# A recurrent attention and a leaky-ReLU layer on one core: the first quad's instructions and loads in a new order

## The chip, the core and the metric

The kernel runs on one core of a Trainium2 chip. The metric is device time in microseconds (us) of one execution, lower is better. The core has five engines with a queue each: TensorE (PE in the profile; its weight loads are shown apart, as PEld), VectorE (DVE), ScalarE (ACT), GpSimd (POOL) and SyncE (SP), which here only issues DMAs. Each queue is worked off in its own order; between queues an instruction waits on semaphores for the data that it reads and for the buffers that it writes.

## What is computed

Four batches of eight heads, 768 steps, head size 48. Each head keeps a 48 x 48 state that decays by a gate and takes up an outer product per step; its outputs, with the heads side by side, are the rows of x (3072 x 384), which go through two matrix products with a leaky ReLU between.

```python
f = 1.0 / (1.0 + np.exp(-f_logit))
for t in range(S):
    state = f[:, :, t, :, None] * state + np.einsum('bhd,bhe->bhde', k[:, :, t], v[:, :, t])
    y[:, :, t] = np.einsum('bhd,bhde->bhe', q[:, :, t], state)
x = y.transpose(0, 2, 1, 3).reshape(B * S, H * D)
h = x @ w_in                      # 384 x 2048
out = np.maximum(0.01 * h, h) @ w_out   # 2048 x 384
```

## The kernel before

The 768 steps are cut into six chunks of 128. A chunk of one batch is a unit (24 of them, number 4c + b); the four units of a chunk are a quad, and all its data for q, k, v and f is loaded at once, 128 partitions of 1536 fp32 values, 768 KB. Within a chunk the recurrence becomes matrix products: running sums of the logarithm of the gate give decay factors; k and q are scaled by them (k by the exponential of the sum, q by that of its negative), turned so that the head dimension lies on partitions (kT and qT), multiplied to scores, masked to a triangle, and multiplied with v; what earlier chunks left is added by a product with the state.

**The stages of a quad**, as the helpers name them:

- gate: `g_exp`, `g_ln` (ACT, two halves of the heads), `g_sum`, `g_cast`, `g_pe` (the sum over partitions on TensorE), `g_add`, then the factors `g_em` and `g_a` (ACT, into the single buffers `em_t` and `a_t`) and `g_end`;
- scaling on DVE: `g_k` and `g_q`; then either DMA moves and DMA transposes (`kq_dma`, `t_dma`) or turns on TensorE (`t_pe`, `t_out`) to kT and qT; v is cast (`cast_v`) and moved (`v_dma`);
- `score_pe`, `mask`, `mix_pe`, `y_out` per unit, and the state: `state_pe`, `state_dve`, `state_pool`;
- x is turned, by `x_pe` and `x_out` (TensorE and a copy) or by `x2_dma` (a DMA transpose of two units);
- the layer: `up4` (three matmuls 128x512 for one of 16 groups of columns of w_in, all four units) with `up4_act` (the leaky ReLU on ACT), and `down` (four matmuls 128x384, a quarter of the sum over 2048) with `put` and the stores. For quad 0 the first product runs in two halves of two units each, as `up` (six matmuls 128x256, two groups of columns) with `up_act`.

**The first quad** has functions of its own, named `q_...` (lines 221 to 323). Its gate sums are made on TensorE with 32-row matmuls (`q_gate32`), the decay factors leave PSUM through ACT (`q_decay_b`, into `emT` and `aT`), k and q are cast and turned unscaled (`q_k_cast`, `q_q_cast`, `q_turn_pe`), and scaled on the way out of PSUM (`q_k_mul`, `q_q_mul`). v is picked into natural order by matmuls (`q_pick`, `q_v_out`). Half of the score blocks go through a DVE mask, the other half through an ACT copy (`q_wf_act`) and a triangle select on POOL (`q_mask_pool`). `idle_pe(n, bank)` issues n matmuls on zeros.

**What sets the order.** Nothing is scheduled by a compiler. Line 60 turns automatic scheduling off, and the calls from line 512 to line 1360 are one list; each engine gets its instructions in the order of this list. The list was found by a search, apart from the calls of the first quad, which stood by hand. The eight PSUM banks are given as numbers in the calls: an operation that fills a bank waits until the last reader of that bank is done.

**Loads and their queues.** f of quad 0 comes in six pieces on the ACT and SP queues; k, q and v of quad 0 on SP (lines 83, 84, 512). All other loads of q, k, v and f are `load_all` on SP, in the order of the list. The weights go through POOL's queue, with a cast from fp32 to bf16: w_in in two halves of its columns (`load_w_in`), w_out in four pieces (`load_w_out`). SP's queue and POOL's queue are served side by side by the same 16 DMA engines. Two helpers hold a queue back: `gate(t, src)` has POOL write one element of a buffer from `src`, so that the load into that buffer comes after it, and `touch(what)` has POOL read one element of a loaded tile, so that POOL goes on only when that load has landed:

```python
gate(fqs[1], v_bs[1][:, 0, 0:1])      # L599: f of quad 1 after the first v of quad 0
touch('q')                            # L532: ahead of both w_in loads on POOL
touch('k1')                           # L665: ahead of w_out pieces 1 to 3 on POOL
```

fqs, kqs and qqs are pairs of buffers, of which quad c uses number c % 2; `v_raws` is one buffer. f of quad 2 goes into the buffer that quad 0 used.

Of the kernel before, what the change touches and what calls it, by code (L numbers as in the profile page):

```python
# [16 lines left out]
def kernel(  # L17
# [10 lines left out]
    nc = tc.nc  # L28
# [55 lines left out]
    load_all(qq, q)  # L84
# [437 lines left out]
    idle_pe(4, 7)  # L522
    q_turn_pe(khq, 0, 4)
    q_decay_b(0, emT, 1.0, 0, 0)
    q_decay_b(1, emT, 1.0, 1, 0)
    q_gate32(1, 0, 1, 2, 3)
    q_decay_b(0, aT, -1.0, 0, 0)
    q_k_mul(0, 0, 0, 4)
    q_turn_pe(khq, 1, 5)
    q_k_mul(0, 1, 0, 4)  # L530
    q_decay_b(3, emT, 1.0, 3)
    touch('q')  # L532
    q_q_cast(V, 1)
# [48 lines left out]
    q_q_mul(1, 1, 1, 6)
    q_pick(2, 7)
    q_v_out(A, 3, 5)
    q_mix_pe(1, 4)
    q_mix_pe(0, 3)
    q_v_out(V, 2, 7)
    q_score_pe(1, 1, 1, 2)
    y_out(A, 1, 4)
    y_out(V, 0, 3)  # L590
    q_back_pe(3, 6)
    state_pe(0, 5)
    q_mask(1, 1, 0, 1)
    q_wf_act(1, 1, 1, 2)
    x_pe(1, 0)
    x_pe(0, 7)
    q_score_pe(0, 1, 4, 3)
    load_w_out(0)
    gate(fqs[1], v_bs[1][:, 0, 0:1])  # L599
    q_back_out(A, 3, 6)  # L600
    x_out(V, 1, 0)
    state_pe(1, 2)
    x_out(V, 0, 7)
    q_back_pe(2, 1)
    q_mask_pool(1, 1, 1)
    q_wf_act(0, 1, 1, 3)
    q_mask(0, 1, 0, 4)
    state_pe(3, 0)
    order_pe(6)
    load_all(fqs[1], f_logit, 1)  # L610
    load_all(kqs[1], k, 1)
    q_state_dve(0)
    up(0, 7, 7)
# [48 lines left out]
    up_act(1, 7, 1)
    up_act(1, 0, 4)
    q_state_pool(3)
    touch('k1')  # L665
    g_sum(V, 1, 2)
    g_sum(V, 1, 3)
    up_act(0, 2, 5)
    up_act(1, 3, 2)
    g_cast(V, 1)  # L670
    g_pe(1, 6)
    g_add(1, 1, 6)
    g_em(1, 1)
    load_w_out(1)
    g_add(1, 0, 6)
    up(1, 6, 1)
    g_a(1, 0)
    down(3, 0, 4)
    g_em(1, 0)
    load_all(fqs[0], f_logit, 2)  # L680
    g_a(1, 1)
    up_act(1, 6, 1)
    load_all(fqs[1], f_logit, 3)
    g_k(V, 1, 2)
    g_k(V, 1, 3)
    g_q(V, 1, 0)
    down(2, 0, 5)
    up(1, 5, 2)
    load_w_out(2)
    load_w_out(3)  # L690
    g_q(V, 1, 1)
    down(1, 1, 7)
    down(0, 1, 3)
    g_end(1, 6)
    up_act(1, 5, 2)
    t_pe(1, 0, 1, 0)
    down(3, 1, 4)
    t_out(A, 1, 0, 1, 0)
    t_pe(1, 1, 0, 6)
    g_k(V, 1, 0)  # L700
    g_k(V, 1, 1)
    t_pe(1, 0, 0, 2)
    t_out(A, 1, 0, 0, 2)
    down(0, 2, 3)
    g_q(V, 1, 3)
    g_q(V, 1, 2)
    t_pe(1, 1, 1, 0)
    t_out(A, 1, 1, 1, 0)
    down(2, 1, 5)
    down(3, 2, 4)  # L710
    t_out(V, 1, 1, 0, 6)
    score_pe(6, 0, 6)
    mask(6, 0, 0)
    mask(6, 1, 6)
    g_exp(2, 1)
    g_exp(2, 0)
    q_state_pool(1)
    cast_v(G, 1, 1)
    q_state_pool(0)
    cast_v(G, 1, 0)  # L720
    v_dma(1, 2)
    v_dma(1, 1)
    score_pe(4, 2, 1)
# [12 lines left out]
    g_ln(2, 1)
    mix_pe(6, 1)
    mask(7, 1, 0)
    g_exp(3, 1)
    v_dma(1, 0)  # L740
    g_ln(2, 0)
    v_dma(1, 3)
# [4 lines left out]
    down(3, 3, 4)  # L747
    mix_pe(4, 2)
    put(A, 1, 7)
    kq_dma(1, 0, 1)  # L750
    y_out(A, 4, 2)
    y_out(A, 6, 1)
    mix_pe(5, 3)
    y_out(A, 5, 3)
    state_pe(5, 7)
    mix_pe(7, 0)
    y_out(A, 7, 0)
    x_pe(4, 2)
    down(2, 3, 5)
    kq_dma(1, 0, 3)  # L760
    kq_dma(1, 0, 2)
    kq_dma(1, 0, 0)
    x_pe(5, 3)
    load_all(kqs[0], k, 2)
    x_out(A, 4, 2)
    x_pe(7, 0)
    x_out(V, 7, 0)
    put(A, 3, 4)
    x_out(A, 5, 3)
    load_all(v_raws[0], v, 2)  # L770
    x_pe(6, 1)
    x_out(V, 6, 1)
    g_ln(3, 1)
    state_pe(4, 2)
    state_pe(6, 6)
    cast_v(G, 2, 0)
    state_dve(4)
    state_pe(7, 4)
    g_pe(2, 0)
    g_add(2, 1, 0)  # L780
    g_exp(3, 0)
    up4(1, 0, 1)
    up4_act(1, 0, 1)
    state_dve(7)
    state_dve(5)
    up4(1, 10, 2)
    state_pool(7)
    cast_v(G, 2, 1)
    up4(1, 1, 3)
    g_em(2, 1)  # L790
    g_add(2, 0, 0)
    up4_act(1, 1, 3)
    g_end(2, 0)
    g_k(V, 2, 2)
    up4(1, 6, 1)
# [24 lines left out]
    up4(1, 15, 6)  # L820
    put(V, 2, 5)
    g_sum(V, 3, 2)
    down(5, 0, 7)
    kq_dma(2, 0, 0)
    up4(1, 8, 2)
    g_q(V, 2, 1)
    g_q(V, 2, 2)
    g_q(V, 2, 0)
    up4_act(1, 4, 3)
    up4(1, 5, 5)  # L830
    up4_act(1, 5, 5)
    up4_act(1, 13, 1)
    up4(1, 14, 0)
    kq_dma(2, 0, 1)
    up4(1, 11, 3)
    g_sum(V, 3, 3)
    up4_act(1, 11, 3)
    g_q(V, 2, 3)
    up4_act(1, 14, 0)
    up4_act(1, 8, 2)  # L840
    up4(1, 9, 5)
    up4_act(1, 9, 5)
    state_pool(4)
    t_pe(2, 1, 0, 1)
    down(4, 0, 3)
    t_out(V, 2, 1, 0, 1)
    t_pe(2, 1, 1, 0)
    t_out(A, 2, 1, 1, 0)
    g_cast(G, 3)
    g_pe(3, 2)  # L850
    g_add(3, 0, 2)
    up4_act(1, 15, 6)
    g_add(3, 1, 2)
    g_a(3, 0)
    g_em(3, 0)
    state_pool(5)
    state_pool(6)
    g_end(3, 2)
    down(4, 1, 3)
    out_dma(2)  # L860
    kq_dma(2, 0, 3)
    kq_dma(2, 0, 2)
    down(5, 1, 7)
    g_a(3, 1)
    g_em(3, 1)
# [24 lines left out]
    load_all(fqs[0], f_logit, 4)  # L890
# [500 lines left out]
```

## Time and profile before

| | us |
|---|---|
| median of three runs | 183.94 |
| lowest and highest run | 181.56, 184.01 |
| the profiled execution | 184.06 |
| its span, from first to last instruction | 182.3 |
| TensorE busy | 169.2 (93% of the span) |
| ACT busy | 116.1 (64%) |
| DVE busy | 108.6 (60%) |
| POOL busy | 49.8 (27%) |
| granted TensorE clock, mean | 0.99 |
| HBM read, written | 25.17 MB, 4.72 MB |

Busy time of TensorE is not work at its peak: the end of a matmul is modelled, and matmuls overlap, so a group of n takes less than n times the mean of one. The chain of waits shows a group at the rate at which it really passes. An instruction that waits is not busy; the trace gives the idle time before it and what ended it. A DMA is shown with its issue (on SPq or POOLq) and the time from issue to landing. In the queries, PE L472 is `up`, L482 `up4`, L490 `down`, L417 the scores, L428 and L431 the two halves of `mix_pe`, L439 `state_pe`, L462 `x_pe`, L399 `t_pe`, L252 `q_pick`; on ACT L477 and L486 are the activations of `up` and `up4`, L328 is `g_exp`; on DVE L267 is `q_k_mul` and `q_q_mul`; L73 is any `load_all`, L179 `load_w_in`, L184 `load_w_out`.

### The profile page before, as it was taken

How to read it: one execution, taken by the hardware profiler on the slowest of the kernel's cores; microseconds unless marked ns; L12 is line 12 of the kernel's file. 1: busy time of each engine (PE TensorE's matmuls, PEld its weight loads, DVE VectorE, ACT ScalarE, POOL GpSimd, SP SyncE). 2: the span in 40 equal slices, each digit the busy share in tenths (PEclk: the TensorE clock that was granted, in tenths of full speed). 3: DMA queues.
4: the chain of work that ended last, by engine and by line, in shares of the span. 5: the costliest groups of instructions: out<-in, count | busy, mean ns of one | idle time of the engine just before them, and what ended most of it. 6: DMA issues, size and time to landing. Idle time of an engine off the chain costs nothing.

```text
span 182.3 us, 3982 instructions
## 1 busy us (share of the span) xinstructions
PE 169.2 (93%) x1546; PEld 107.4 (59%) x1546; DVE 108.6 (60%) x229; ACT 116.1 (64%) x211; POOL 49.8 (27%) x99
## 2 busy tenths in 40 slices
PE   7589999939999999979989999999999999999992
PEld 5375889717584555665545675556755566555561
DVE  7679942892699789759566895666780057400020
ACT  2878498955898999385987179861566921076302
POOL 8377205630015333001840176120006500000000
PEclk9999999978999999999999999999999999999999
DMA  5998999999797058998698797889477884371004
GB/s 157 309 234 155 210 296 327 312 217 327 212 338 231 29 170 154 329 330 246 205 139 185 235 331 253 187 156 324 110 192 249 172 208 137 61 281 64 4 0 173
DMA packets 55171, 37.61 MB, mean 206 GB/s; under 512 B 19569, under 2 KB 53873, under 8 KB 55153
## 3 DMA queue, kind: packets, MB, share of 16 engines
q1 hardware_dynamic: 53216, 33.82, 65.8%
q0 software_dynamic: 1376, 3.15, 9.7%
q10 hardware_dynamic: 560, 0.39, 0.7%
q8 instruction: 12, 0.20, 0.5%
q14 instruction: 7, 0.05, 0.1%
HBM read 25.17 MB, written 4.72 MB: 164 GB/s over the span
## 4 chain that ended last, share of the span: by engine, by line
PE 63%; DMA 22%; ACT 5%; SPq 3%; DVE 3%; POOL 1%; issue 1%; DVEq 0%; ACTq 0%; POOLq 0%
PE ps L490 29%; PE ps L482 24%; DMA kq<-in_k_dram 15%; DMA w_out_b<-in_moe_w_out_dram 5%; PE ps L417 3%; DMA kTs<-kh 3%; ACT gT L238 2%; PE ps L431 2%; PE ps L428 2%; PE ps L399 2%; PE ps L439 1%; PE ps L462 1%; SPq L392 1%; SPq L382 1%; SPq L69 1%
## 5 line engine op out<-in xcount | busy, mean ns | idle before, releaser
L490 PE MATMUL ps<-w_out_b,gT 128*128 128x384 bf16 x384 | 71.9, 330 | 2.9 <-DMA w_out_b<-in_moe_w_out_dram 2.9
L486 ACT ACTIVATE gT<-ps 128x512 bf16<-128x512 f32 x80 | 44.6, 606 | 19.2 <-PE ps L482 18.3
L482 PE MATMUL ps<-xQ,w_in 128*128 128x512 bf16 x240 | 54.4, 379 | 0.6 <-ACT gT L486 0.6
L490 PEld LDWEIGHTS <-gT 128*128 128x128 bf16 x384 | 35.4, 98 | 25.4 <-issue 4.1
L482 PEld LDWEIGHTS <-w_in 128*128 128x128 bf16 x240 | 26.8, 113 | 23.4 <-issue 0.8
L421 DVE TENSOR_TENSOR wm<-ps,ut 128x512 bf16<-128x512 f32 x40 | 25.3, 684 | 22.0 <-PE ps L417 21.6
L147 ACT CAST xn<-ps 128x384 bf16<-128x384 f32 x20 | 9.0, 485 | 21.8 <-PE ps L431 19.5
L149 DVE COPY osb<-ps 128x384 f32<-128x384 f32 x11 | 5.9, 554 | 23.2 <-PE ps L490 21.2
L320 POOL CAST sb<-sf 64x192 bf16<-64x192 f32 x40 | 16.2, 404 | 9.7 <-DVE sf L314 5.6
L453 POOL TENSOR_TENSOR sf<-sf,a_end 128x192 f32<-128x192 f32 x16 | 9.6, 600 | 30.8 <-PE ps L482 15.8
L149 POOL CAST vQ<-v_raw 128x768 bf16<-128x768 f32 x9 | 7.6, 847 | 20.0 <-DMA qh<-qhQ 18.0
L368 DVE TENSOR_TENSOR khQ<-kq,em_t 128x384 bf16<-128x384 f32 x20 | 11.3, 600 | 2.5 <-DMA kq<-in_k_dram 2.0
L147 ACT COPY osb<-ps 128x384 f32<-128x384 f32 x13 | 6.1, 486 | 10.2 <-PE ps L490 10.2
L472 PE MATMUL ps<-xQ,w_in 128*128 128x256 bf16 x96 | 12.1, 273 | 0.2
L368 DVE TENSOR_TENSOR qhQ<-qq,a_t 128x384 bf16<-128x384 f32 x20 | 11.8, 619 | 0.3 <-DMA qq<-in_q_dram 0.3
L336 DVE TENSOR_TENSOR fq<-fq 128x384 f32<-128x384 f32 x15 | 8.6, 572 | 5.5 <-ACT fq L332 5.2
L472 PEld LDWEIGHTS <-w_in 128*128 128x128 bf16 x96 | 10.2, 114 | 1.1 <-issue 0.7
L352 DVE TENSOR_TENSOR fq<-fq,ps 128x768 f32<-128x768 f32 x10 | 9.4, 953 | 2.3 <-PE ps L346 1.8
L328 ACT ACTIVATE fq<-fq 128x768 f32<-128x768 f32 x10 | 8.3, 851 | 0.7 <-DMA fq<-in_f_logit_dram 0.7
L360 ACT ACTIVATE a_t<-fq 128x768 bf16<-128x768 f32 x10 | 8.5, 853 | 0.0
L356 ACT ACTIVATE em_t<-fq 128x768 bf16<-128x768 f32 x10 | 8.5, 851 | 0.0
L477 ACT ACTIVATE gT<-ps 128x512 bf16<-128x512 f32 x16 | 8.3, 600 | 0.0
(98 smaller groups left out, 188.3 us busy)
## 6 DMA issues: line engine op xcount, KB each, us to landing
kq<-in_k_dram SPq DMA_DIRECT2D x6, 768.0 KB, 7.2
qq<-in_q_dram SPq DMA_DIRECT2D x6, 768.0 KB, 9.8
fq<-in_f_logit_dram SPq DMA_DIRECT2D x5, 768.0 KB, 9.5
v_raw<-in_v_dram SPq DMA_DIRECT2D x5, 768.0 KB, 7.3
out_dram<-osb SPq DMA_DIRECT2D x4, 768.0 KB, 4.6
kh<-khQ SPq DMA_DIRECT2D x20, 128.0 KB, 3.6
v_b<-vQ SPq DMA_DIRECT2D x20, 96.0 KB, 2.2
w_in<-in_moe_w_in_dram POOLq DMA_DIRECT2D x2, 768.0 KB, 9.3
```

What stands on the lines that cost most here:

```text
L147: eng.copy(out=out, in_=in_)
L149: eng.tensor_copy(out=out, in_=in_)
L320: nc.gpsimd.tensor_copy(out=state_b[b][r, :, e * D:(e + 1) * D], in_=state_f[b][r])
L336: eng.tensor_add(t[:, :, j, :], t[:, :, j, :], t[:, :, j - 1, :])
L352: nc.vector.tensor_add(t, t, x[:, :, None, :].to_broadcast([128, 4, 4, D]))
L368: eng.tensor_mul(out.rearrange("p (j g) d -> p j g d", j=4)[:, :, h, 0:D], raw[:, h].rearrange("p e j d -> p j e d"), by[:, h].rearrange(" ...
L421: nc.vector.tensor_mul(wms[e][u % R_WM], bank(bk).rearrange("p (i n) -> p i n", i=P2), ut[:, None, :].to_broadcast([128, P2, 128]))
L453: nc.gpsimd.tensor_mul(sf, sf, a_ends[c % 2][:, :, b:b + 1].to_broadcast([128, P2, D]))
L472: nc.tensor.matmul(bank(bk)[:, i * 256:(i + 1) * 256].rearrange("p (a n) -> p a n", a=2), w_in_p[ff // 8][:, kk, ff // 4 % 2, :, ff % 4], ...
L482: nc.tensor.matmul(bank(bk).rearrange("p (a n) -> p a n", a=B), w_in_p[ff // 8][:, kk, ff // 4 % 2, :, ff % 4], xQs[c % R_XT][:, :, kk, :] ...
L486: nc.scalar.activation(g_piece(c, ff), bank(bk), AF.Prelu, alpha=0.01)
L490: nc.tensor.matmul(bank(bk)[:, 0:KD], g_part(u, ff), w_out_b[:, ff, :], start=(ff == 0), stop=(ff == NF - 1))
```

## The change

The whole list of calls is replaced by another one, in which the calls of the first quad stand in a searched order too. The set of operations stays nearly the same; apart from the order, bank numbers change, and some copies and casts change their engine. What differs in kind:

- Loads of quad 0 go in the order k, v, q. After them come f of quad 1 and f of quad 2, which stood far later in the list; k, q and v of quad 1 follow.
- The gate ahead of f of quad 1 reads `ident`, a constant, and not the first v. `touch('k')` takes the place of `touch('q')`; `touch('k1')` is gone.
- w_in is loaded in four quarters of its columns, in the order 0, 2, 1, 3. Of w_out, piece 1 is loaded first, then 0, 2 and 3.
- `g_exp` of quad 1, first half, stands on ACT ahead of the four `q_wf_act`; the gate work of quads 1 and 2 runs up to their sums while `up` of quad 0 runs.
- All four `q_mix_pe` stand ahead of the first `up`; before, two of them did.
- `idle_pe` issues 58 matmuls, where before it issued 36.
- x of quad 3 is turned by two `x2_dma`, where before by four `x_pe` and `x_out`.
- The description of the change also says that q of quad 2 is turned on TensorE. In both lists that is two calls `t_pe(2, 1, ...)`; the list of before has them on lines 844 and 846.

The diff, cut to its core:

```diff
     load_all(kq, k)
-    load_all(qq, q)
...
     def load_w_in(g):
-        w = FF // 2
-        nc.gpsimd.dma_start(out=w_in_b[g],
+        w = FF // 4
+        nc.gpsimd.dma_start(out=w_in_b[g // 2][:, :, g % 2 * w:g % 2 * w + w],
                             in_=moe_w_in.rearrange("(a p) n -> p a n", p=128)[:, :, g * w:(g + 1) * w])
...
     load_all(vq, v)
+    load_all(qq, q)
+    idle_pe(24, 7)
     q_exp_act(0)
+    q_exp_act(1)
     q_ln_act(0)
-    q_exp_act(1)
-    idle_pe(24, 7)
+    idle_pe(15, 7)
     q_gate32(0, 0, 1, 2, 3)
     q_ln_act(1)
+    gate(fqs[1], ident[:, 0:1])
+    touch('k')
+    q_gate32(1, 0, 1, 2, 3)
     q_k_cast(V, 0)
-    q_k_cast(G, 1)
+    load_all(fqs[1], f_logit, 1)
...
+    load_all(fqs[0], f_logit, 2)
...
+    q_v_cast(G, 0)
+    q_decay_b(3, emT, 1.0, 3, None)
+    q_decay_b(2, emT, 1.0, 2, None)
...
+    q_v_cast(A, 1)
+    idle_pe(12, 7)
+    q_pick(0, 4)
...
+    load_w_in(0)
+    q_decay_b(0, aT, -1.0, 0, 1)
+    q_q_cast(G, 0)
+    q_pick(1, 6)
+    load_w_in(2)
...
+    q_pick(2, 3)
+    q_q_cast(V, 1)
     q_decay_b(0, aT, -1.0, 0, 0)
     load_w_in(1)
     q_k_mul(1, 1, 0, 5)
+    q_turn_pe(qhq, 1, 1)
+    q_back_pe(0, 4)
+    q_back_out(A, 0, 4)
+    q_v_out(V, 1, 6)
+    load_w_in(3)
...
+    g_exp(1, 0)
+    load_w_out(1)
+    q_pick(3, 6)
+    q_q_mul(0, 1, 0, 0)
+    q_score_pe(1, 0, 4, 5)
+    q_wf_act(1, 0, 1, 5)
...
+    q_mix_pe(2, 0)
+    load_w_out(0)
+    load_all(kqs[1], k, 1)
...
+    x_pe(2, 0)
+    up(0, 1, 7)
+    g_exp(1, 1)
+    g_ln(1, 0)
```

More of the change, by code (lines that the diff above doesn't have):

```diff
@@ L585 @@
+    q_mask(0, 1, 0, 0)
+    state_pe(0, 2)
+    q_back_pe(2, 3)
+    q_mask_pool(0, 0, 1)
     q_mix_pe(1, 4)
-    q_mix_pe(0, 3)
-    q_v_out(V, 2, 7)
-    q_score_pe(1, 1, 1, 2)
+    q_mix_pe(0, 7)
+    q_back_pe(1, 5)
     y_out(A, 1, 4)
[L590 to L595, printed above, removed]
-    x_pe(0, 7)
[L597 to L601, printed above, removed]
@@ L664 @@
+    g_ln(2, 0)
+    g_sum(V, 1, 2)
+    q_state_dve(3)
     q_state_pool(3)
-    touch('k1')
-    g_sum(V, 1, 2)
     g_sum(V, 1, 3)
[L668 to L711, printed above, removed]
@@ L738 @@
[L738 to L742, printed above, removed]
+    g_cast(G, 1)
     g_sum(V, 2, 1)
@@ L762 @@
+    mask(7, 1, 2)
     kq_dma(1, 0, 0)
-    x_pe(5, 3)
-    load_all(kqs[0], k, 2)
[L765 to L769, printed above, removed]
+    down(3, 3, 6)
+    put(A, 3, 6)
+    score_pe(6, 5, 4)
+    mask(6, 0, 5)
+    down(2, 3, 7)
+    put(A, 2, 7)
+    mix_pe(4, 6)
+    y_out(A, 4, 6)
+    mix_pe(7, 2)
+    mix_pe(5, 7)
+    state_pe(7, 6)
+    load_all(fqs[1], f_logit, 3)
+    x_pe(4, 5)
+    mask(6, 1, 4)
+    mix_pe(6, 4)
+    down(0, 3, 1)
+    y_out(V, 7, 2)
@@ new lines @@
+    y_out(A, 5, 7)
+    x_out(A, 4, 5)
+    x_pe(5, 5)
+    x_pe(7, 7)
+    g_em(2, 1)
+    y_out(V, 6, 4)
+    x_pe(6, 4)
+    x_out(A, 6, 4)
+    load_all(kqs[0], k, 2)
+    g_exp(3, 0)
+    down(1, 3, 3)
+    state_pe(5, 2)
+    put(A, 1, 3)
+    x_out(V, 5, 5)
+    x_out(V, 7, 7)
+    up4(1, 5, 4)
+    up4(1, 10, 7)
+    g_ln(3, 0)
+    up4_act(1, 10, 7)
+    up4(1, 6, 3)
+    up4_act(1, 6, 3)
+    g_exp(3, 1)
+    state_dve(5)
+    up4(1, 14, 2)
+    up4_act(1, 14, 2)
+    put(V, 0, 1)
+    g_k(V, 2, 0)
@@ L770 @@
+    g_k(V, 2, 1)
+    load_all(qqs[0], q, 2)
+    up4(1, 0, 7)
     load_all(v_raws[0], v, 2)
-    x_pe(6, 1)
-    x_out(V, 6, 1)
+    up4(1, 3, 3)
     g_ln(3, 1)
-    state_pe(4, 2)
-    state_pe(6, 6)
+    up4(1, 15, 1)
+    g_k(V, 2, 2)
+    g_k(V, 2, 3)
+    cast_v(G, 2, 1)
     cast_v(G, 2, 0)
-    state_dve(4)
[L778 to L783, printed above, removed]
+    kq_dma(2, 0, 0)
+    kq_dma(2, 0, 1)
+    kq_dma(2, 0, 3)
+    g_q(V, 2, 0)
@@ L830 @@
[L830 to L853, printed above, removed]
+    t_out(V, 2, 1, 0, 4)
@@ L917 @@
[L917 to L940 removed]
+    mask(11, 1, 2)
+    score_pe(10, 4, 7)
```

1298 lines of the change are left out of this document (647 added, 651 removed).

## The prediction

> **What bounds the kernel now.** I read the chain of waits first, then TensorE's timeline, then the table of waits, then the DMA answers for the first 45 us.
>
> ```profile
> PE 63%; DMA 22%; ACT 5%; SPq 3%; DVE 3%; POOL 1%; issue 1%; DVEq 0%; ACTq 0%; POOLq 0%
> ```
> The chain that ends last is TensorE work with DMA time between. So I split TensorE's time at marks that both orders share.
>
> ```profile
> 21.02 1.64 PE L472 MATMUL ps<-xQ,w_in 128*128 128x256 bf16 x12
> ...
> 26.48 4.75 PE L472 MATMUL ps<-xQ,w_in 128*128 128x256 bf16 x42
> ...
> 39.25 2.72 PE L490 MATMUL ps<-w_out_b,gT 128*128 128x384 bf16 x8 [2.86 <-DMA w_out_b<-in_moe_w_out_dram]
> ...
> 54.82 4.06 PE L482 MATMUL ps<-xQ,w_in 128*128 128x512 bf16 x18
> ...
> 172.88 6.01 PE L490 MATMUL ps<-w_out_b,gT 128*128 128x384 bf16 x36
> ```
> The marks are: first `up` at 21.02, first `up4` at 54.82, last matmul at 172.88 + 6.01 = 178.89. The span of 182.3 ends 3.41 us after that (last copy, last store). The profiled run took 184.06, so 1.76 lies outside the span; 184.06 is at the upper end of the three runs (181.56 to 184.01, median 183.94), but only 0.1 from their median, so the sum can be held against either.
>
> TensorE waits after the first `up` are few:
>
> ```profile
> PE ps L462 <- DVE xQ L149: 1.0, 1, 1.0
> PE ps L417 <- DMA kTs<-kh: 0.7, 1, 0.7
> PE ps L482 <- ACT gT L486: 0.6, 1, 0.6
> ```
> These are 2.3 us, all after 54.82. The largest is the 2.86 us above, and it costs more than itself, because the granted clock falls behind it (stretch, its length, busy time of TensorE, its weight load, DVE, ACT and POOL, then granted clock, DMA share, GB/s):
>
> ```profile
> 40.00:42.00 2.00, 2.00 (x10) 0.97 (x8) 0.63 (x2) 0.00 (x0) 0.00 (x0) 0.50 1.04 229
> 42.00:44.00 2.00, 2.00 (x28) 1.74 (x27) 0.14 (x1) 1.01 (x1) 0.00 (x0) 0.92 1.08 360
> ```
> Clock 0.50 from 40 to 42: eight `down` matmuls take 2.72 there, against 1.30 for eight in the rows of term 4, so 1.4 lost. Wait and clock together are 4.3 us.
>
> **Term 1, the w_out wait.** Its cause stands on POOL:
>
> ```profile
> 30.46 0.19 POOL L175 COPY seen<-kq 128x1 f32<-128x1 f32 x1 [1.69 <-DMA kq<-in_k_dram]
> 30.92 1.62 POOL L184 DMA_DIRECT2D w_out_b<-in_moe_w_out_dram x3 [0.28 <-issue]
> ```
> ```profile
> DMA to landing us min/median/max: 8.3/9.6/11.4
> ```
> `touch('k1')` held three w_out pieces until k of quad 1 landed; the first then needs 8.3 us, 30.92 + 8.3 = 39.2, exactly where TensorE starts again. The last, issued near 32.0, lands 11.4 later at 43.4: three pieces of 384 KB, some 2.1 us apart. In the new order no touch stands there. Piece 1 follows the w_in quarters at about 16.5 us, piece 0 follows POOL's four triangle selects, pieces 2 and 3 come near 30 and 33 and are first needed after six `down` parts. The 4.3 us go, unless transfers queue.
>
> **Term 2, what the transfers now do.** The SP queue of before:
>
> ```profile
> 3.00 0.66 SPq L73 DMA_DIRECT2D qq<-in_q_dram  x1
> 4.49 1.93 SPq L73 DMA_DIRECT2D gT<-in_v_dram  x1
> 17.59 0.60 SPq L73 DMA_DIRECT2D fq<-in_f_logit_dram  x1
> ```
> ```profile
> qq<-in_q_dram SPq DMA_DIRECT2D x1, 768.0 KB, 8.2
> ...
> gT<-in_v_dram SPq DMA_DIRECT2D x1, 768.0 KB, 9.0
> ...
> fq<-in_f_logit_dram SPq DMA_DIRECT2D x1, 768.0 KB, 10.3
> ```
> After k, q lands at 3.00 + 8.2 = 11.2 and v at 4.49 + 9.0 = 13.5, so a load takes 2.3 us once the queue runs. In the order k, v, q, v takes q's place at 11.2 and q takes v's at 13.5. Then the gate on f of quad 1 waited for v's first output (17.59); now it waits only for `ident`, so f1 follows q directly, and f2 (behind the first logarithms), k1, q1 and v1 are no longer held. They meet w_in:
>
> ```profile
> 16.00:18.00 2.00, 2.00 (x14) 1.20 (x13) 2.00 (x6) 1.30 (x4) 1.57 (x4) 1.00 1.11 201
> 20.00:22.00 2.00, 2.00 (x29) 1.62 (x26) 1.96 (x7) 0.83 (x2) 1.09 (x2) 1.00 1.13 214
> 26.00:28.00 2.00, 2.00 (x23) 1.99 (x21) 0.71 (x2) 1.27 (x4) 0.68 (x2) 1.00 1.10 350
> ```
> w_in alone moves 201 GB/s, fp32 loads alone 350; the mix moves 214 at 20 us, so there the loads get under a fifth. In that mix f1 took 10.3 us. Now most of f1 moves before w_in starts (POOL waited for q ahead of w_in and waits for k and v now; with half of v to cast, w_in leaves it at about 12; its data starts an estimated 1.5 us later), so I take its landing at 16.2, with ends 16 and 24 (rival 2). A w_in quarter has the bytes of a w_out piece, so 2.1 us each undisturbed, and 3 if the loads beside it get a third (I take this between the fifth just read and a half): landings near 18.5, 21, 24, 27, then w_out pieces 1 and 0 near 29 and 31.5. The `up` parts run in the quarters' order 0, 2, 1, 3 and need them from 22, 23.5, 25.5 and 27.5; w_out piece 0 is needed near 32. So nothing waits, but the last two margins are under a microsecond.
>
> The Trainium skill, "DMA: Bandwidth & Descriptors", section "Anatomy of one DMA", gives each such transfer a fixed 2 us beside its bytes, which speaks against quarters; taken as serial, two more transfers would add 4 us to w_in and make the sum 182.7 (rival 3). The trace disagrees: the pieces 2.1 us apart above leave no room for a serial 2 us.
>
> **Term 3, the head up to the first `up`.** Prices of queued work:
>
> ```profile
> 30.91 4.03 ACT L477 ACTIVATE gT<-ps 128x512 bf16<-128x512 f32 x8
> ```
> ```profile
> 27.95 1.58 ACT L328 ACTIVATE fq<-fq 128x768 f32<-128x768 f32 x2 [0.72 <-DMA fq<-in_f_logit_dram]
> ```
> ```profile
> 12.83 1.07 DVE L267 TENSOR_TENSOR qTs<-ps,gT 128x256 bf16<-128x256 bf16 x3
> ```
> ```profile
> 15.60 2.77 PE L252 MATMUL ps<-gT 128*128 128x384 bf16 x16
> ```
> So back to back 0.50 per 512-wide ACT operation, 0.75 per 768-wide, 0.35 per turn product on DVE, 0.66 per `q_pick`. q lands at 13.5 instead of 11.2, and now the q products are last: POOL and DVE cast q (by 14.8), TensorE has three picks (2.0) ahead of the q turns, which end near 16.2. Eight products (2.8) and four masks on DVE reach 20; ACT has `g_exp(1,0)` of f1, four score copies, `y_out`, `q_v_out`, `q_back_out`, `y_out` behind it, 0.75 + 8 x 0.5 = 4.8 from 16.2 to 21. All four mixes come first, where before only two did. First `up` at 22.2; ends 21.4 (no pick in the way) and 23.3 (no overlap on DVE). The 22 extra fillers stand ahead of steps that wait for ACT or v; without that cover the 15 behind the first 24 delay the gates by some 0.7 us, but ACT then waits for v at 11.2 in any case: its own half of the v cast stands ahead of six decays, and those are what the last k products and the q products need.
>
> **Term 4, `up` to `up4`.** Pipelined prices from the chain of waits:
>
> ```profile
> 101.42 0.17 PE ps L439 x4
> 101.59 1.30 PE ps L490 x8
> 102.89 0.17 PE ps L428 x4
> 103.06 0.20 PE ps L431 x8
> 103.26 0.33 PE ps L417 x8
> ...
> 105.74 0.17 PE ps L462 x3
> ```
> An `up` is 4.75 / 7 = 0.66 (less the last one's tail). 16 `up` 10.6, 16 `down` 10.4, four `t_pe` of eight transposes 1.8 (at a third of 0.17 each), four scores 1.3, four mixes 1.5, five `x_pe` 0.9, three `state_pe` 0.5, two `g_pe` 0.5: 27.5 us. ACT's list for the `up` stretch (16 activations, six f operations, four decays) is 16 x 0.5 + 10 x 0.75 = 15.5 from 22, so it ends near 38 and keeps step with TensorE. Waits for banks and for w_out piece 0: between 0 and the old 2.86; I take 1.4, the middle, since ACT is full there. First `up4`: 22.2 + 27.5 + 1.4 = 51.1, against 54.82.
>
> **Term 5, the rest.** 178.89 - 54.82 = 124.1. Four `x_pe` of quad 3 become DMA transposes: -0.7, covered by ten `down` parts, 6.5 us. Two `state_pe` more: +0.3. The old waits: -2.3. So 121.4. New waits of the same kind: a `mask` or `x_out` queued on DVE behind a `g_k`, v of quad 5 loaded late, bank reuse. I take 1.5, between 0 and somewhat over twice the old 2.3. The words on q of quad 2 cost nothing: before already has both `t_pe(2, 1, ...)`.
>
> **Sum.** 51.1 + 121.4 + 1.5 + 3.4 = 177.4, plus 1.76: 179.2 us, 2.6% below the median. By the ends of terms 3 to 5 it is 176.3 to 182; nearly all the gain lies in terms 1 and 5.
>
> **Rivals.** 1, new waits eat the gain. For it: the order is new to its last line, and an order with few waits on paper still showed four here. Against it: loads of later quads are issued 7 us or more ahead of use. With 4 to 5 us in term 5 and 2.9 in term 4: 183 to 184. Chance 0.23.
>
> 2, slower: f1 lands late. `g_exp(1, 0)` stands on ACT ahead of the four score copies, so nothing of quad 0 passes it. The first `up` follows f1's landing by 4.8 plus a turn and a copy, 5.3; it decides from a landing at 16.9, and the gain is gone from 21.7. The rows from 20 to 22 us speak for it, the late start of w_in against. If w_in goes ahead wholly from 13.5, f1 lands near 13.5 + 4 x 2.1 + 2.3 = 24.2: 179.2 + 7.3 = 186.5, and a clock drop of the size above makes 188. Chance 0.13 (0.09 beyond 2%).
>
> 3, quarters pay their fixed part: the last quarter near 31, 3.5 us late for its `up`: 182.7. Chance 0.04, by the 2.1 us spacing.
>
> The forecast keeps 0.60, its own range 177 to 181.5.
>
> **Numbers.** A measurement of this kernel tells about 2%: below 180.26 is faster, above 187.62 slower. Of the forecast's 0.60, 0.45 lie below 180.26; the rest with rivals 1, 3 and the milder part of 2 makes 0.46 within 2%; slower 0.09. Range 176.8 to 184.4: it leaves out the worse half of rival 2 and a little on each side.
>
> **What would show it.** Right: no TensorE wait on w_out near 36 and clock 1.00 there; f1 landed by 17; first `up` by 23 and first `up4` by 52. Wrong: ACT idle before the exponential of f1 (rival 2), TensorE waiting for w_in or w_out between 25 and 35 (term 2), or waits after 52 that total over 4 us (rival 1).

## The result and the profile after

| | before | after |
|---|---|---|
| median, us | 183.97 (4 runs) | 188.10 (4 runs) |
| lowest and highest | 181.56, 184.47 | 187.26, 188.82 |
| ratio after to before | | 1.0285, 95% interval 1.0225 to 1.0345 |
| profiled execution, and its span | 184.06, 182.3 | 188.82, 187.1 |
| first `up` | 21.02 | 21.91 |
| first `up4` | 54.82 | 59.26 |
| first `up4` to the end of the last matmul | 124.07 | 124.04 |

The change makes the kernel slower by 2.9%. A time here and below is the median of all executions of a kernel, while a ratio leaves out those that ran in the chip's slower state. The marks of the prediction, laid on both traces, say where: up to the first `up` the new order is 0.9 us behind (forecast: 1.2); the stretch from there to the first `up4` is 3.5 us longer (37.35 against 33.80); from there to the end of the last matmul it is the same to 0.03 us, and the tail behind it is 0.4 longer. The helpers stand one line higher after the change, so `up` is L471, `up4` L481, `down` L489.

TensorE's timeline of the changed kernel, with start, length, engine, line, operation, count, and in brackets the idle time ahead of it and what ended that:

```profile
21.91 0.27 PE L471 MATMUL ps<-xQ,w_in 128*128 128x256 bf16 x1
27.22 1.25 PE L471 MATMUL ps<-xQ,w_in 128*128 128x256 bf16 x5 [5.04 <-DMA w_in<-in_moe_w_in_dram]
...
28.59 5.59 PE L471 MATMUL ps<-xQ,w_in 128*128 128x256 bf16 x30
...
41.52 2.76 PE L489 MATMUL ps<-w_out_b,gT 128*128 128x384 bf16 x16 [1.25 <-ACT gT L476]
...
59.26 1.03 PE L481 MATMUL ps<-xQ,w_in 128*128 128x512 bf16 x4
...
177.94 5.36 PE L489 MATMUL ps<-w_out_b,gT 128*128 128x384 bf16 x32
```

The first group has six matmuls. One of them runs at 21.91; the other five stand for 5.04 us until a piece of w_in lands. The windows of the same trace (stretch, length, busy time of TensorE, weight load, DVE, ACT and POOL, then granted clock, DMA share and GB/s):

```profile
22.00:24.00 2.00, 0.18 (x3) 0.00 (x0) 1.57 (x5) 2.00 (x4) 0.00 (x0) 1.00 1.17 234
24.00:26.00 2.00, 0.00 (x0) 0.00 (x0) 0.00 (x0) 0.60 (x1) 0.00 (x0) 1.00 1.19 231
26.00:28.00 2.00, 0.78 (x4) 0.59 (x5) 0.00 (x0) 0.00 (x0) 0.00 (x0) 0.51 1.17 232
28.00:30.00 2.00, 2.00 (x13) 1.35 (x10) 1.13 (x4) 1.49 (x3) 0.00 (x0) 0.50 1.16 236
30.00:32.00 2.00, 2.00 (x11) 1.31 (x10) 1.56 (x4) 1.43 (x2) 0.00 (x0) 0.50 1.07 223
32.00:34.00 2.00, 2.00 (x16) 1.74 (x15) 0.00 (x0) 0.00 (x0) 0.00 (x0) 0.78 1.06 273
...
38.00:40.00 2.00, 2.00 (x23) 1.80 (x21) 1.75 (x3) 1.09 (x3) 1.87 (x6) 1.00 0.00 0
```

Behind the wait the clock is 0.50 for some six microseconds, so the loss is larger than the wait. While TensorE stands, the DMA engines are full (share 1.17 to 1.19, 231 to 234 GB/s); from 38 to 40 they do nothing. Some of what moved beside w_in was not yet needed: k of quad 1, issued at 11.16, is first read at 42.7. Who issued what: the POOL queue, and below it the SP queue, both of the changed kernel.

```profile
12.10 0.95 POOL L178 DMA_DIRECT2D w_in<-in_moe_w_in_dram  x1
13.78 1.21 POOL L148 CAST qhQ<-qq 128x768 bf16<-128x768 f32 x1 [0.73 <-DMA qq<-in_q_dram]
14.93 2.33 POOL L178 DMA_DIRECT2D w_in<-in_moe_w_in_dram  x3
```

```profile
11.16 2.25 SPq L73 DMA_DIRECT2D kq<-in_k_dram  x1
13.45 3.77 SPq L73 DMA_DIRECT2D qq<-in_q_dram  x1
17.26 7.61 SPq L73 DMA_DIRECT2D v_raw<-in_v_dram  x1
```

And from issue to landing, the tile w_in of the changed kernel:

```profile
DMA to landing us min/median/max: 9.0/10.3/13.7
```

The quarters go in the order 0, 2, 1, 3 and are issued at 12.10, 14.93, 15.71 and 16.48. The first takes 9.0, the last 13.7; the second takes 9.1, and the median of the four, 10.3, then gives the third 2 x 10.3 - 9.1 = 11.5. So they land at 21.1, 24.0, 27.2 and 30.2. The first `up` group, `up(0, 1)`, reads columns of quarter 0 alone, and that was there since 21.1. It went on at 27.22, when quarter 1 had landed. That is the riddle that the experiments start from.

### The profile page after: what moved, and what is told of

The parts are those of the page before. It is cut to its first block, busy times and chain, and to the rows that moved or that the text cites. A ratio compares the mean times of both kernels' runs of the same rounds, so it can differ in the third digit from the quotient of the medians.

```text
span 187.1 us, 4020 instructions
## 1 busy us (share of the span) xinstructions
PE 172.7 (92%) x1556; PEld 108.9 (58%) x1556; DVE 111.5 (60%) x229; ACT 116.8 (62%) x209; POOL 49.4 (26%) x98
## 4 chain that ended last, share of the span: by engine, by line
PE 56%; DMA 29%; SPq 4%; DVE 3%; POOL 3%; issue 1%; ACT 1%; POOLq 0%; DVEq 0%; ACTq 0%
PE ps L489 28%; PE ps L481 15%; DMA qq<-in_q_dram 8%; DMA w_in<-in_moe_w_in_dram 6%; PE ps L471 4%; DMA v_raw<-in_v_dram 3%; DMA kTs<-kh 3%; PE ps L416 3%; DMA qTs<-qh 3%; DMA v_b<-vQ 2%; DMA kh<-khQ 2%; SPq L386 2%; DMA fq<-in_f_logit_dram 2%; PE ps L430 2%; SPq L391 1%
## 5 line engine op out<-in xcount | busy, mean ns | idle before, releaser
L489 PE MATMUL ps<-w_out_b,gT 128*128 128x384 bf16 x384 | 70.0, 326 | 1.3 <-ACT gT L476 1.3
L481 PE MATMUL ps<-xQ,w_in 128*128 128x512 bf16 x240 | 55.3, 379 | 0.3 <-ACT osb L146 0.3
L489 PEld LDWEIGHTS <-gT 128*128 128x128 bf16 x384 | 35.0, 98 | 23.6 <-issue 1.4
L481 PEld LDWEIGHTS <-w_in 128*128 128x128 bf16 x240 | 26.5, 113 | 22.2 <-issue 0.5
L148 DVE COPY osb<-ps 128x384 f32<-128x384 f32 x7 | 3.9, 556 | 27.1 <-PE ps L489 23.6
L471 PE MATMUL ps<-xQ,w_in 128*128 128x256 bf16 x96 | 14.6, 310 | 5.0 <-DMA w_in<-in_moe_w_in_dram 5.0
L146 ACT CAST xn<-ps 128x384 bf16<-128x384 f32 x15 | 7.0, 482 | 17.0 <-PE ps L430 16.7
L146 ACT COPY osb<-ps 128x384 f32<-128x384 f32 x17 | 8.2, 483 | 12.8 <-PE ps L489 11.1
L471 PEld LDWEIGHTS <-w_in 128*128 128x128 bf16 x96 | 11.0, 122 | 7.3 <-DMA w_in<-in_moe_w_in_dram 5.7
L148 POOL CAST vQ<-v_raw 128x768 bf16<-128x768 f32 x7 | 6.5, 940 | 31.6 <-DMA v_raw<-in_v_dram 31.5
L335 DVE TENSOR_TENSOR fq<-fq 128x384 f32<-128x384 f32 x15 | 10.1, 678 | 0.6 <-ACT fq L331 0.2
L140 PE MATMUL ps<-fill 128*128 128x256 bf16 x58 | 9.3, 326 | 1.1 <-DVE fill L97 1.1
L416 PE MATMUL ps<-qTs,kTs 64*128 64x128 bf16 x160 | 7.6, 218 | 1.8 <-DMA qTs<-qh 1.1
L416 PEld LDWEIGHTS <-kTs 64*128 64x128 bf16 x160 | 4.5, 94 | 8.1 <-issue 6.9
## 6 DMA issues: line engine op xcount, KB each, us to landing
w_in<-in_moe_w_in_dram POOLq DMA_DIRECT2D x4, 384.0 KB, 10.3
```

The costliest lines, as they stand in the source:

```text
L146: eng.copy(out=out, in_=in_)
L148: eng.tensor_copy(out=out, in_=in_)
L335: eng.tensor_add(t[:, :, j, :], t[:, :, j, :], t[:, :, j - 1, :])
L416: nc.tensor.matmul(bank(bks[e])[:, p * 128:(p + 1) * 128], kTs[c % 2][r, b, p], qTs[c % 2][r, b, p], start=True, stop=True)
L471: nc.tensor.matmul(bank(bk)[:, i * 256:(i + 1) * 256].rearrange("p (a n) -> p a n", a=2), w_in_p[ff // 8][:, kk, ff // 4 % 2, :, ff % 4], ...
L481: nc.tensor.matmul(bank(bk).rearrange("p (a n) -> p a n", a=B), w_in_p[ff // 8][:, kk, ff // 4 % 2, :, ff % 4], xQs[c % R_XT][:, :, kk, :] ...
```

## The experiments

**Theory A.** A tile of w_in holds two quarters beside each other in each of three blocks (kk = 0, 1, 2) of 1024 columns. Quarter 1 is written to columns 512 to 1023 of each block, so its first and last address enclose quarter 0 of the blocks kk = 1 and 2. A matmul that reads there waits for quarter 1 as well, though it reads none of it; kk = 0 of quarter 0 lies ahead of that range and doesn't wait. One matmul ran, five waited. **Rival:** the transfers alone are late, and a group waits for its own quarter. Then k, q and v of quad 1 beside w_in are the cause. The first four runs are meant to separate the two (the expectations call the rival theory B). Each ratio is to runs of the kernel before on the same chip at the same time (medians 183.05 to 183.75).

`e1_four_tiles`: each quarter a tile of its own.

```diff
-    w_in_b = [const.tile([128, NK, FF // 2], ...) for i in range(2)]
+    w_in_b = [const.tile([128, NK, FF // 4], ...) for i in range(4)]
...
-        nc.gpsimd.dma_start(out=w_in_b[g // 2][:, :, g % 2 * w:g % 2 * w + w],
+        nc.gpsimd.dma_start(out=w_in_b[g],
...
```

> The changed kernel with w_in as four tiles of 512 columns each instead of two tiles of 1024; loads, order and every matmul operand are the same data. Theory A (the first up waits for a quarter that it does not read: matmuls two and three of a group read columns that lie inside the address range of the neighbour quarter's write, and that quarter was loaded third): the 5.0 us wait of TensorE on w_in goes, the second up group waits at most about 1 us for its own quarter, the granted clock stays 1.00 from 26 to 34 us, first up4 near 53 instead of 59.3, time about 182. Theory B (the transfers are slow because five loads run beside them, and the quarter itself came late): nothing changes, 188.

`e2_hold_k1`: the two tiles as they are, but k of quad 1 (and q and v behind it on SP) held until the second v output of quad 0.

```diff
     load_w_out(0)
+    gate(kqs[1], v_bs[1][:, 0, 0:1])
     load_all(kqs[1], k, 1)
```

> The changed kernel with one more gate on POOL, after the second w_out piece: k, q and v of quad 1 are issued at about 21 us instead of 11, so that from 14 to 21 us only f of quads 1 and 2 runs beside w_in. Theory A: the third quarter still decides, but lands at about 23 to 24 instead of 27.2, the wait shrinks to 1.5 to 2.5 us, time 183 to 185. Theory B: the quarter that is read lands early enough, no wait, time about 182. If the loads take little from w_in: unchanged, 188.

`e3_both`: both edits.

> Four tiles and the gate together. Theory A: no wait on w_in beyond 0.5 us, but little is added to the four tiles alone, 181 to 182. Theory B: as the gate alone. If k of quad 1 comes late through the gate, TensorE waits near 40 us and it is worse than the four tiles alone.

`e4_halves`: w_in in two halves, at the places of the first two quarter loads.

> The changed kernel with w_in in two halves as before (issued at the places of the first two quarters); everything else as changed. Theory A: the first two up groups run with the first half, landed by about 21; the third group (second half) waits until 24 to 26, 1 to 3 us; time 183 to 185. Theory B: the halves compete with the same loads, wait as long as now or longer, 187 to 189.

| | time, us | ratio to before (95%) | w_in waits | first `up4` | from there to the last matmul's end |
|---|---|---|---|---|---|
| after | 188.10 | 1.0285 (1.0225 to 1.0345) | 5.04 | 59.26 | 124.04 |
| e1 | 183.23 | 1.003 (0.999 to 1.007) | 1.95 | 53.57 | 123.87 |
| e2 | 185.21 | 1.011 (1.004 to 1.017) | 3.62 | 55.53 | 123.91 |
| e3 | 183.14 | 1.000 (0.996 to 1.004) | 0 | 51.43 | 125.81 |
| e4 | 187.40 | 1.021 (1.014 to 1.028) | 3.42 | 58.07 | 123.73 |

TensorE's timeline of `e1_four_tiles`:

```profile
22.00 0.82 PE L471 MATMUL ps<-xQ,w_in 128*128 128x256 bf16 x6
22.82 0.82 PE L471 MATMUL ps<-xQ,w_in 128*128 128x256 bf16 x6
23.81 2.15 PE L471 MATMUL ps<-xQ,w_in 128*128 128x256 bf16 x18 [0.17 <-DMA w_in<-in_moe_w_in_dram]
27.16 0.85 PE L471 MATMUL ps<-xQ,w_in 128*128 128x256 bf16 x6 [1.19 <-DMA w_in<-in_moe_w_in_dram]
...
30.07 1.50 PE L471 MATMUL ps<-xQ,w_in 128*128 128x256 bf16 x12 [0.59 <-DMA w_in<-in_moe_w_in_dram]
```

The groups now wait at about 24, 27 and 30, each for its own quarter, in the order of landing; no stop is long, the clock stays at 1.00, and the ratio to before falls from 1.0285 to 1.003 although the quarters land as late as they did. Holding the loads alone (`e2`) ends the first wait at 25.20 instead of 27.22: the landing is earlier, and the wait for the wrong quarter stays. It stays in the second tile too: one matmul of `up(0, 5)` runs, the next waits 0.88 us for the last quarter. Theory A explains most: the tiles alone bring the first `up4` from 59.26 to 53.57, both edits bring it to 51.43. The load beside w_in is the second part.

Not all went as expected. The times of theory A were too low: 183.2 in `e1` (expected 182), 185.2 in `e2` (183 to 185), 183.1 in `e3` (181 to 182). In `e4` the first two groups run on the first half, as theory A says, but the second half landed at 27.5 and not between 24 and 26; the wait was 3.42 us instead of 1 to 3, and the time, 187.4, is what the rival gave. So `e4` doesn't separate the two; `e1` and the next run do.

`e8_order` asks theory A for something it has not been fitted to: the two tiles, quarters in the order 0, 1, 2, 3.

```diff
-    load_w_in(2)
+    load_w_in(1)
...
-    load_w_in(1)
+    load_w_in(2)
```

> The changed kernel, two tiles as they are, with the quarters loaded in the order 0, 1, 2, 3 instead of 0, 2, 1, 3. Theory A (a quarter's matmul waits for the other quarter of its tile as well): the first group's second matmul waits from 22 for the second load (landed 24.0 in the changed kernel), 2 us, and the first group of the second tile, up(0, 5), then waits for the last load (30.2), 4 to 5 us; 6 to 7 us of waits in two places, and the first up4 no earlier than 59. Rival (each group waits for its own quarter alone): no wait for the first two groups, one wait of about 3.5 us for the third load (27.2), first up4 at about 56, time about 186.

Its TensorE timeline:

```profile
21.86 0.27 PE L471 MATMUL ps<-xQ,w_in 128*128 128x256 bf16 x1
24.63 1.26 PE L471 MATMUL ps<-xQ,w_in 128*128 128x256 bf16 x5 [2.50 <-DMA w_in<-in_moe_w_in_dram]
26.00 1.70 PE L471 MATMUL ps<-xQ,w_in 128*128 128x256 bf16 x7
30.35 4.37 PE L471 MATMUL ps<-xQ,w_in 128*128 128x256 bf16 x23 [2.65 <-DMA w_in<-in_moe_w_in_dram]
```

Twice the same picture: one matmul of a tile's first group runs (the seventh of the x7 is the first of `up(0, 5)`), then TensorE stops until the neighbour quarter is in, 24.63 and 30.35. The first stop ends with quarter 1 whether it is loaded third (after the change) or second (here), so it doesn't go by the number of loads that have landed. First `up4` at 59.79, time 189.79, ratio 1.033 (1.025 to 1.041): theory A's numbers, and not the rival's 56 and 186, bar the second wait. That is 2.65 where 4 to 5 was expected (both waits 5.15 for 6 to 7), because the first wait ended 0.6 us later than forecast and half clock behind it stretched the twelve matmuls between.

**Where e3's gain goes.** `e3_both` reaches the first `up4` at 51.43, 3.4 us ahead of before, and still takes the time of before: its rest is 1.74 us longer. Two rows of its TensorE timeline, the wait in the `up` stretch and the first one behind `up4`:

```profile
33.69 2.76 PE L489 MATMUL ps<-w_out_b,gT 128*128 128x384 bf16 x16 [1.25 <-ACT gT L476]
...
54.01 5.99 PE L481 MATMUL ps<-xQ,w_in 128*128 128x512 bf16 x27 [1.12 <-ACT osb L146]
```

The second row is `up4(1, 6)`, which needs the bank that `put(A, 1, 3)` empties; on ACT that copy stands behind `g_exp(3, 0)`, which waits for f of quad 3. ACT's timeline of `e3_both`, with the `a_end` row that sets the first wait, and then its SP queue:

```profile
32.97 0.18 ACT L362 ACTIVATE a_end<-ps 128x16 f32<-128x16 f32 x1 [1.40 <-DVE fq L351]
...
52.75 0.84 ACT L327 ACTIVATE fq<-fq 128x768 f32<-128x768 f32 x1 [1.46 <-DMA fq<-in_f_logit_dram]
```

```profile
42.96 3.05 SPq L381 DMA_DIRECT2D v_b<-vQ  x4
46.06 1.25 SPq L386 DMA_DIRECT2D kh<-khQ  x2
47.40 0.64 SPq L73 DMA_DIRECT2D fq<-in_f_logit_dram  x1
48.09 0.67 SPq L73 DMA_DIRECT2D kq<-in_k_dram  x1
```

The loads of f 3 and k 2 are free to go from 38 (their buffers were read last by then), but SP works in order, and ahead of them stand four copies of v of quad 1, which wait for v itself. The next three runs are edits on `e3_both`.

`e5_end_first`:

```diff
     g_pe(1, 3)
+    g_end(1, 3)
...
-    g_end(1, 3)
...
     g_pe(2, 2)
+    g_end(2, 2)
     g_add(2, 1, 2)
-    g_end(2, 2)
```

> e3_both with g_end(1, 3) and g_end(2, 2) moved directly behind g_pe(1, 3) and g_pe(2, 2), ahead of the g_add that reads the same bank. Theory: the 1.25 us for which TensorE waits ahead of down(3, 0) in e3_both comes from ScalarE, where g_end(2, 2) stands 1.40 us behind VectorE's g_add(2, 1) and holds up_act(1, 2); with g_end ahead both waits are under 0.4 us, the first up4 starts at about 50.3 instead of 51.43, and the span is about 180.0 (time 182). Rival: the loads of f 3 and k 2, which SyncE issues behind the copies of v of quad 1, set when the first up4 groups go on, so the gain comes back as a longer wait of ScalarE for f 3 (1.46 us in e3_both, then about 2.5) and the span stays within 0.4 us of 181.1.

`e6_loads_first`:

```diff
     kq_dma(1, 0, 1)
+    load_all(fqs[1], f_logit, 3)
+    load_all(kqs[0], k, 2)
...
-    load_all(fqs[1], f_logit, 3)
...
-    load_all(kqs[0], k, 2)
```

> e3_both with the loads of f 3 and k 2 moved on SyncE to stand behind the second kq_dma of quad 1, ahead of the copies of v, so that they are issued at about 38.4 and 39.1 instead of 47.40 and 48.09. Theory: f 3 and k 2 land before 47, the waits of ScalarE for f 3 (1.46 us) and of VectorE for k 2 (2.07 us) go, TensorE's wait of 1.12 us ahead of the up4 group behind put(A, 1, 3) goes with them, and the span is 179 to 180 (time about 181). Rival: the transfer rate is what binds there; v of quad 1 lands 1 to 2 us behind its 41.3, the copies of v and with them the first mix of quad 1 come later by as much, and the span stays within 0.5 us of 181.1 or above it.

`e7_all`: both.

> Both edits of e5_end_first and e6_loads_first on e3_both. If the two waits are in line with one another, as the chain of e3_both has them, the gains add: span 178 to 179, time about 180, under the 183.2 of the kernel before by 1.5%. If the later one absorbs the earlier one, the span is that of e6_loads_first within 0.4 us.

| | time, us | ratio to before (95%) | first `up4` | rest |
|---|---|---|---|---|
| e5 | 182.75 | 0.995 (0.991 to 0.9999) | 52.18 | 126.26 |
| e6 | 181.73 | 0.990 (0.982 to 0.998) | 51.90 | 124.18 |
| e7 | 181.32 | 0.986 (0.977 to 0.995) | 52.39 | 124.19 |
| e12 | 180.31 | 0.985 (0.980 to 0.991) | 51.18 | 124.04 |

In `e5` the wait of 1.25 is gone, and its rival was right too: ACT waits 1.83 for f of quad 3 instead of 1.46, TensorE 1.50 behind it. (Its profiled execution, 183.94, was the longest of ten, with q of quad 0 late in the head; hence the late 52.18.) In `e6` the two loads go out at 38.44 and 39.12, the waits of ACT for f 3 and of DVE for k 2 are gone, and the rest is back at the 124.1 of before. It costs a little where its rival said: the first mix of quad 1 now waits 0.42 us for v. Both edits together beat both kernels, by 1.4 to 1.5% against before, and `e12_all_again`, the same kernel as `e7`, confirms it. Whether the two gains add is not settled: the profiled span is 180.4 in `e7`, about that of `e6` (179.9), and 179.0 in `e12`, as it would be if they add.

> The kernel e7_all unchanged, in more runs, since its four runs lay between 180.22 and 182.94. If the gain is the kernel's own, the ratio to the kernel before is 0.983 to 0.992 again (time 180.5 to 182) and the interval leaves out 1. If it depended on those few runs, as a late landing of q in the head (a wait of 1.4 us in the profiled one) would make it, the ratio is 0.995 or above.

TensorE's timeline of `e12_all_again`:

```profile
21.90 0.82 PE L471 MATMUL ps<-xQ,w_in 128*128 128x256 bf16 x6
22.72 3.44 PE L471 MATMUL ps<-xQ,w_in 128*128 128x256 bf16 x30
...
47.31 0.36 PE L430 MATMUL ps<-v_b,wm 128*128 128x48 bf16 x8 [0.99 <-DMA v_b<-vQ]
51.18 7.29 PE L481 MATMUL ps<-xQ,w_in 128*128 128x512 bf16 x33
```

`e9_before_w_out` tests term 1 alone, on the kernel before.

```diff
     load_w_out(0)
+    load_w_out(1)
     gate(fqs[1], v_bs[1][:, 0, 0:1])
...
-    load_w_out(1)
```

> The kernel before with one edit: load_w_out(1) moved from behind touch('k1') to directly behind load_w_out(0), so that piece 1 of w_out is issued at about 17.4 us instead of 30.9. Theory (term 1 of the prediction by itself): the wait of 2.86 us at 39.25 and the half clock behind it go, the first up4 comes 4.3 us earlier, at about 50.5, and the span falls from 182.3 to about 178 (ratio 0.977). Rival: as in e3_both, the loads issued later on SyncE set when the first up4 groups go on, and f of quad 1, with which piece 1 now shares the transfers, lands 1 to 2 us later; then the first up4 is at 51.5 to 53 and the span at 180 or above (ratio 0.99 to 1).

Time 182.99, ratio 0.998 (0.993 to 1.003); first `up4` 53.45, span 180.8. Three rows of `e9_before_w_out`, of its SP queue, of ACT and of TensorE:

```profile
18.52 0.60 SPq L73 DMA_DIRECT2D fq<-in_f_logit_dram  x1
```

```profile
30.52 1.58 ACT L328 ACTIVATE fq<-fq 128x768 f32<-128x768 f32 x2 [2.91 <-DMA fq<-in_f_logit_dram]
```

```profile
34.58 0.82 PE L472 MATMUL ps<-xQ,w_in 128*128 128x256 bf16 x6 [2.32 <-ACT gT L477]
```

The w_out wait is gone, and f of quad 1 is used at 30.52 instead of 27.95, so that an `up` waits 2.32 us for its bank behind ACT. Of the 2.6 us by which f is later, 0.9 is its issue (18.52 instead of 17.59: the gate stands on POOL behind the added issue, and this execution was 0.4 behind already), and 1.7 the longer transfer beside piece 1 (12.0 us instead of 10.3). Of 4.3 us there remain 1.4 at the first `up4` and 1.5 in the span of the profiled executions; the ratio can't be told from 1. The rival held, though its first `up4` was to be at 51.5 to 53.

Two more edits were meant to better `e7_all`, and both made it worse. `e10_no_gate` leaves out the gate on k 1:

```diff
     load_w_out(0)
-    gate(kqs[1], v_bs[1][:, 0, 0:1])
     load_all(kqs[1], k, 1)
```

> e1_four_tiles (no gate on k 1) with the two edits of e7_all: g_end ahead of g_add, and the loads of f 3 and k 2 ahead of the copies of v. Theory: without the gate the w_in waits of e1_four_tiles stay (2.0 us in all), but v of quad 1 lands at about 38 to 39 instead of 41 to 43, so the waits of the first mixes for v (1.0 to 1.6 us in e6_loads_first and e7_all) go; the two about cancel and the time is that of e7_all, 181 to 182, ratio 0.985 to 0.99. Rival: the first up4 alone decides; then it is 1.5 to 2 us behind e7_all, ratio 0.995 or above.

184.68, ratio 1.007 (1.003 to 1.011); first `up4` 54.77. The w_in waits are back (2.2 us), and the first mix waits 1.12 us for v (0.42 in `e6`, 0.99 in `e12`; the other part of the 1.0 to 1.6 that the expectation names lies at 150 us and has nothing to do with it). v lands earlier, but its copies still stand on SP behind f 3 and k 2 and are issued at 42.59, only 0.4 ahead of the 42.98 of `e12`. The theory that the two cancel fell, and the rival (0.995 or above) held.

`e11_k2_behind` puts k 2 behind the copies of v:

```diff
-    load_all(kqs[0], k, 2)
...
     v_dma(1, 1)
+    load_all(kqs[0], k, 2)
```

> e7_all with the load of k 2 behind the copies of v of quad 1 instead of ahead of them; f 3 stays ahead. Theory (the transfers bind there: what is issued ahead delays what stands behind it): the copies of v no longer share with k 2, TensorE's waits for them fall from 1.6 us to under 0.8, k 2 is issued at about 46.5 and lands near 53, ahead of VectorE's use at 54 to 55; time 180.5 to 181.3, ratio 0.982 to 0.986. Rival: f 3 is the one that delays v, or k 2 at 46.5 lands behind its use as in e3_both (a wait of VectorE of over 1 us); then the time is that of e7_all or above, ratio 0.986 to 0.99.

186.80, ratio 1.014 (1.006 to 1.021). The reason stands in its TensorE timeline, and one view down in its SP queue:

```profile
51.52 0.34 PE L438 MATMUL ps<-v_b,kh 128*128 128x96 bf16 x4 [3.76 <-DMA kh<-khQ]
```

```profile
42.91 2.46 SPq L381 DMA_DIRECT2D v_b<-vQ  x4
45.42 0.64 SPq L73 DMA_DIRECT2D kq<-in_k_dram  x1
46.10 1.32 SPq L386 DMA_DIRECT2D kh<-khQ  x2
```

The waits of quad 1 for v are gone, as meant. But the copies of scaled k (128 KB each), one of which a state product needs at 47.8, were now issued 0.7 us behind 768 KB and took 5.2 us to land (median of the two), where in `e12`, behind the copies of v, they took 2.1. Neither theory had named them.

## Why the prediction was wrong

| mark | forecast | measured | off by |
|---|---|---|---|
| first `up` (term 3) | 22.2 | 21.91 | -0.3 |
| `up` to `up4` (term 4, with 1 and 2) | 28.9 | 37.35 | +8.4 |
| `up4` to the last matmul's end (term 5) | 122.9 | 124.04 | +1.1 |
| tail, and outside the span | 5.2 | 5.5 | +0.4 |
| time | 179.2 | 188.82 | +9.6 |

**The step that failed** is the end of term 2: "The `up` parts run in the quarters' order 0, 2, 1, 3 and need them from 22, 23.5, 25.5 and 27.5 ... So nothing waits". Two things in it were wrong.

- It took for granted that a group waits for its own quarter. It waits for the neighbour in its tile too (`e1`, `e8`). Undoing that alone, with a tile for each quarter, brings the first `up4` from 59.26 to 53.57.
- The landings. Their spacing was right (3 us forecast, 2.9 to 3.2 measured), their start was not: 21.1, 24.0, 27.2, 30.2 for 18.5, 21, 24, 27. The estimate let the four follow one another on POOL from 12 us; in fact POOL waits for q and casts it between the first and the second (13.78, above), and k, q and v of quad 1 take their share. With groups that wait only for their own quarter this costs the 1.95 us of `e1`; with those loads held as well, nothing (`e3`). There the quarters land at 21.0, 23.0, 24.9 and 27.4: the last 2.8 us sooner, the first no sooner. What made the first 2.6 us later than forecast was not tested.

The 8.4 us are 5.04 of wait, 2.85 of half clock (36 matmuls take 0.27 + 1.25 + 5.59 here, 0.82 + 3.44 in `e12`), and 0.5 that remains. TensorE waiting for w_in between 25 and 35 was one of the signs by which the prediction said it would be wrong. It knew that the margins were thin ("under a microsecond") and carried a clock loss in before's own wait, but put a price on a late w_in only in rival 3.

**Term 1** was right in its mechanism: with piece 1 loaded early TensorE doesn't wait on w_out, after the change or in `e9`. Its 4.3 us are not what the edit is worth by itself: in the order of before it delays f of quad 1 and brings 1.4. In the new order f of quad 1 goes ahead, and `e3` has its first `up4` at 51.43 where 51.1 was forecast, so there the size can't be faulted.

**Term 3** held: f of quad 1 was used from 16.89, after 0.68 us of waiting on ACT, and the first `up` came 0.3 ahead of forecast.

**Term 4** held without its surroundings: 37.35 - 5.04 - 2.85 = 29.46, and 29.43 in `e3`, against 28.9. The 1.4 allowed for a bank were 1.25, the one wait behind `g_end`.

**Term 5** was too low by 1.1. The waits of TensorE after the first `up4`:

```profile
PE ps L416 <- DMA qTs<-qh: 1.1, 1, 1.1
PE ps L416 <- DMA kTs<-kh: 0.7, 1, 0.7
PE ps L430 <- DMA v_b<-vQ: 0.4, 1, 0.4
PE ps L481 <- ACT osb L146: 0.3, 1, 0.3
```

These are 2.4 where 1.5 was taken, about what before had (2.3). So the new list is no better there than the old one. In `e3`, where the `up` stretch is within 0.5 us of the forecast, the rest takes 125.81, 2.9 over term 5: with the w_in waits mended the time is 183.1, not 179.2. It takes the edits of `e7` as well to come to 180.3 (`e12`).

**The ends of the sum**, 176.3 to 182, don't follow from the terms. With the lowest and highest values of terms 3 to 5 it comes to 175.5 and about 185, and the measured time lies above that too.

**The rivals.** Rival 2 was the one on the slower side, and it did not happen: f 1 landed at 16.8, just ahead of the 16.9 from which it would have cost. Rival 1, new waits behind a good head, was not what made the kernel slow, but `e3` shows it as soon as the head is mended: 1.74 us of its 3.4 are given back, TensorE waits 4.0 us in all after the first `up4` (the rival: 4 to 5), and the time is 183.1 (183 to 184). Rival 3 came nearest in the landing: the last quarter was in at 30.2 (forecast there: 31). That `e1` then takes 183.2 (forecast there: 182.7) is luck, since its waits on w_in are 1.95 us and not 3.5, and the rest of the difference lies in other terms. For the price of quarters `e4` gives a measure. Its POOL queue, and then the stop of TensorE for the second half:

```profile
11.55 0.95 POOL L178 DMA_DIRECT2D w_in<-in_moe_w_in_dram  x1
...
14.34 0.79 POOL L178 DMA_DIRECT2D w_in<-in_moe_w_in_dram  x1
```

```profile
27.54 5.31 PE L471 MATMUL ps<-xQ,w_in 128*128 128x256 bf16 x24 [3.42 <-DMA w_in<-in_moe_w_in_dram]
```

The second half landed 16.0 us after the first issue (11.55 to 27.54), the last of four quarters 18.1 after it (12.10 to 30.2): quarters cost 2.1 us here. The 4 us that the prediction had estimated from the Trainium skill, "DMA: Bandwidth & Descriptors", section "Anatomy of one DMA", are not reached. Nor are quarters free, as the prediction's own sum had them. The last quarter is issued 4.4 us after the first one and the second half 2.8 after the first; whether these 1.6 us make the difference, or the smaller transfers, stays open.

## What to carry to other kernels

When a load is cut into pieces so that work can start on the first, check which piece each reader really waits for: pieces interleaved in one tile can wait for one another, and a tile per piece avoids it (`e1`). Where the DMA engines are full, a load that is moved ahead is paid by what stands behind it (`e9`, `e11`); ask of each edit which transfer becomes later, and who waits for that one, small copies included. A forecast that rests on margins under a microsecond at full DMA should price the miss with its clock loss, here 5.0 us of wait and 2.9 of clock.

## What the runs showed that was not expected

- A matmul waited 5.04 us for data that it doesn't read, in a pattern (one of six runs, five wait) that follows the address range of a strided write. That a reader waits for the other quarter of its tile is shown by `e1` and `e8`; that the address range is what sets this is inferred from the one and the five, and no run shows that rule itself.
- The clock does not follow the length of a wait alone. It fell to about half behind waits of 5.04 (after), 3.76 (`e11`), 3.42 (`e4`), 2.86 (before), 2.65 and 2.50 (`e8`; behind the 2.50 granted 0.54 from 24 to 26 and 0.60 from 26 to 28), and not behind 2.74 (`e2`) or 2.32 (`e9`), where the windows behind have 1.00. The Trainium skill, "TensorE: Matmul & The Clock Gate", Part 1, has the slow clock come after an idle window of some 3.4 us that runs freely. Three of the waits that were enough here are shorter than that window, and the measurement decides.
- A copy of 128 KB issued 0.7 us behind a load of 768 KB landed about 5 us after its issue (`e11`), behind other small copies 2.1 us after it (`e12`); TensorE stood 3.76 us for the late one.
